# Three visits of 5, 4 and 5 attention chunks for two quads of heads, in place of four of 4, 3, 4 and 3

## The chip, the core and the metric

The kernel runs on one core of a Trainium2 chip. The metric is the device time of one launch in microseconds (us), the median of several runs. Engines are named as the profile names them: PE is TensorE (matmuls), DVE is VectorE, ACT is ScalarE, POOL is GpSimd, SP is SyncE, which here only issues transfers.

## What is computed

A sigmoid attention feeds a gated feed-forward layer. Eight batches of twelve heads, 448 positions, head width 64; the layer is 768 to 1536 to 768.

```python
scores = (1.0 / np.sqrt(64)) * np.matmul(q, k.transpose(0, 1, 3, 2)) - np.log(448)
attn = 1.0 / (1.0 + np.exp(-scores))
attn_out = np.matmul(attn, v)                        # (8, 12, 448, 64)
x = attn_out.transpose(0, 2, 1, 3).reshape(3584, 768)
g = x @ w_gate
out = (g * sigmoid(g) * (x @ w_val)) @ w_out
```

The sigmoid has no sum over a row, so a piece of the attention needs nothing from its neighbours. The kernel works on **quads**: four heads of one batch, 24 quads in all, three to a batch. The 448 keys of a quad are cut into seven **chunks** of 64. For a chunk, TensorE makes the scores of the four heads (`qk_tile`, four matmuls of 64x64 weights and 448 columns), and ScalarE takes their sigmoid (`sig_tile`). When all seven are there, TensorE multiplies them with the values (`pv`, 28 matmuls) and VectorE copies the result out as the layer's input.

## The kernel before

All matmul results go through four PSUM tiles of two banks each, handed out in turn: whoever asks next gets the tile that was handed out four requests ago, and must wait until that tile's last user has been read.

```python
ring = [psD.tile([128, 2, 512], FP32, tag=f"D{i}", name=f"ps_D{i}") for i in range(4)]

class Banked:
    def __init__(self, user=None, at=None, made=None):
        if at is None:
            at = ring_at[0] % 4
            ring_at[0] += 1
        k = ring_order[at]
        self.t = ring[k]
    # write(ins, bank) / read(ins, bank): say that an instruction touches one bank only,
    # so that it need not wait for the readers of the other one
```

Scores and their sigmoid. The score matmuls do not go through `write`, so the first of them waits until both banks of the tile have been read. A sigmoid can be split by bank, so that the next user of the tile gets its first bank sooner.

```python
def qk_tile(n, c, at=None):
    sd = Banked(at=at)
    ...
    for w in range(2):
        for h2 in range(2):
            nc.tensor.matmul(out=sc[w * 64:(w + 1) * 64, h2, :S], ...)     # 64x64 weights
    return sd

def sig_tile(n, c, sd, split=False):
    pt = pt_a[:, pt_at[0] % 10]
    if split:
        for h2 in range(2):
            sd.read(nc.scalar.activation(out=pt[:, h2, :], in_=sc[:, h2, :S], func=SIGM, ...), h2)
    else:
        nc.scalar.activation(out=pt, in_=sc[:, :, :S], func=SIGM, ...)
```

The product with the values takes a tile of the ring as well, and it too waits for both banks. Its three copies to `xT` run on VectorE (with `how` = 1, one of them on ScalarE).

```python
def pv(n, how=0, at=None):
    P = Banked(at=at).t
    for c in range(C):
        for h2 in range(2):
            for w in range(2):
                nc.tensor.matmul(out=P[g:g + 64, h2, :S], lhsT=vt[...], rhs=pts of (n, c), ...)
    first = nc.vector.tensor_copy(out=x, in_=P[:, 0, :S])
    ...
    done = [nc.vector.tensor_copy(out=o, in_=i) for o, i in halves[how:]]
```

Between the visits to the attention TensorE works on the layer. One `ffn1` is one slice of 128 of the 1536 columns for one batch: six matmuls for the gate into bank 0, six for the value into bank 1, then ScalarE and VectorE in a row.

```python
def ffn1(b, f):
    D = Banked("f", made=(b // 2, f))
    ffn1_mm(D, b, f, ...)                  # 6 matmuls gate -> bank 0, 6 matmuls value -> bank 1
    ffn1_gate(D, b, f)
    if b % 2:
        h_sums(b // 2, f)
        make_sums(budget[(b, f)])          # up to `budget` further sums on VectorE
    for fn in fill.pop((b, f), ()):        # further VectorE work in batches 4 and 5
        fn()

def ffn1_gate(D, b, f):
    s16 = ...; D.read(nc.scalar.activation(out=s16, in_=D.t[:, 0, :S], func=SIGM), 0)            # "s"
    t1 = ...;  D.read(nc.vector.tensor_tensor(out=t1, in0=D.t[:, 0, :S], in1=s16, op=MULT), 0)   # "t"
    D.read(nc.vector.scalar_tensor_tensor(out=hT[...], in0=D.t[:, 1, :S], ..., in1=t1, ...), 1)  # "hT"
```

The second half of the layer is `ffn2` (24 matmuls of 384 columns) and `ffn2_group` (42 of them). The last batches use `double`, a form with fewer matmuls, after the attention is over. `fill` puts `fast_w` and `x_sums`, VectorE work that prepares it, behind the `ffn1` of batches 4 and 5.

A **visit** is a group of chunks done together: the scores of its first two, then `pv` of a quad that was completed in an earlier visit, then the rest.

```python
visits = [tiles[:2], tiles[2:4]]
for i in range(0, len(tiles), C):
    visits += [tiles[i:i + 4], tiles[i + 4:i + C]] if i else [tiles[4:C]]

def attn_step(group, pvs, how):
    for part in (group[:2], group[2:]):
        scs = [(n, c, qk_tile(n, c)) for n, c in part]
        rest = [pv(pvs.pop(0), how) for _ in range(len(pvs))]
        for i, (n, c, sc) in enumerate(scs):
            sig_tile(n, c, sc, split=len(group) == 4 and part[0] == group[0] and i == 1)
        for f in rest:
            f()
```

A list of units (`ffn1`, `ffn2`, ...) with their estimated lengths is walked through, and a visit is put in when its planned time is reached and the last visit lies far enough back. `plan` hangs the loads, casts and transposes of later quads on chunks of earlier ones.

Of the kernel before, what the change touches and what calls it, by code (L numbers as in the profile page):

```python
# [20 lines left out]
def kernel(  # L21
# [13 lines left out]
    B, H, S, D = q.shape  # L35
    DM = H * D
    DFF = moe_w_gate.shape[1]
    C = S // D
    NJ = H // 4
    NP = H // 2  # L40
    NF = DFF // 128
    NQ = B * NJ
# [190 lines left out]
    def qk_tile(n, c, at=None):  # L233
        sd = Banked(at=at)
        sc = sd.t
        qt, kt = qT[(n, 0)], qT[(n, 1, c)]
        for w in range(2):
            for h2 in range(2):
                r = slice(h2 * 64, h2 * 64 + 64)
                nc.tensor.matmul(  # L240
                    out=sc[w * 64:(w + 1) * 64, h2, :S],
                    lhsT=kt[r, w * 64:(w + 1) * 64],
                    rhs=qt[r, :, w * 64:(w + 1) * 64],
                    start=True,
                    stop=True,
                )
        return sd

    def sig_tile(n, c, sd, split=False):
        sc = sd.t  # L250
        pt = pt_a[:, pt_at[0] % 10]
        pt_at[0] += 1
        if split:
            for h2 in range(2):
                sd.read(
                    nc.scalar.activation(out=pt[:, h2, :], in_=sc[:, h2, :S], func=SIGM, bias=sbias, scale=qkscale), h2
                )
        else:
            nc.scalar.activation(out=pt, in_=sc[:, :, :S], func=SIGM, bias=sbias, scale=qkscale)  # L259
        pts[(n, c)] = pt  # L260

    def pv(n, how=0, at=None):

        b, j = divmod(n, NJ)
        P = Banked(at=at).t
        vt = v16.pop(n)
        for c in range(C):
            pt = pts.pop((n, c))
            for h2 in range(2):
                for w in range(2):  # L270
                    r = slice(w * 64, w * 64 + 64)
                    g = (w ^ h2) * 64
                    nc.tensor.matmul(  # L273
                        out=P[g:g + 64, h2, :S],
                        lhsT=vt[r, h2, c * D:(c + 1) * D],
                        rhs=pt[r, h2, :],
                        start=(c == 0),
                        stop=(c == C - 1),
                    )

        def x_tile(h2):
            if n >= NQ - NJ:
                at = 4 * W2 + (2 * j + h2) * S
                return half_of(stg_a)[:, at:at + S]
            return xtp.tile([128, S], FP16, tag="xT", name=f"xT_{b}_{2 * j + h2}")

        x = x_tile(0)
        first = nc.vector.tensor_copy(out=x, in_=P[:, 0, :S])  # L288
        xT[(b, 2 * j)] = x
        x = x_tile(1)  # L290
        xT[(b, 2 * j + 1)] = x
        halves = [(x[w * 64:(w + 1) * 64, :], P[(1 - w) * 64:(2 - w) * 64, 1, :S]) for w in range(2)]
        done = [nc.vector.tensor_copy(out=o, in_=i) for o, i in halves[how:]]  # L293
        if how == 2:
            for o, i in halves:
                apart(nc.scalar.copy(out=o, in_=i), first)

        def rest():
            if how == 1:
                o, i = halves[0]  # L300
                apart(nc.scalar.copy(out=o, in_=i), first, *done)

        return rest
# [197 lines left out]
    budget = {}  # L501
# [10 lines left out]
    def make_sums(most):  # L512
        for _ in range(min(most, len(sumq))):
            pb, i, f, kind = sumq.pop(0)
            h1 = hT[(pb, f)].rearrange("p b s -> p (b s)")
            a11, a21 = h1[:, :GT], h1[:, GT:2 * GT]
            if kind in (1, 4):
                h2 = hT[(pb, f + FW)].rearrange("p b s -> p (b s)")
                a12, a22 = h2[:, :GT], h2[:, GT:2 * GT]
            t = htp.tile([128, GT], FP16, tag=f"S{kind}_{i}", bufs=1, name=f"S{kind}_{pb}_{i}")  # L520
            hS[(pb, kind, i)] = t
            if kind == 1:
                a, b, op = a21, a22, ADD
            elif kind == 2:
                a, b, op = hS[(pb, 1, i)], a11, SUB
            elif kind == 3:
                a, b, op = a11, a21, SUB
            else:
                a, b, op = a12, hS[(pb, 2, i)], SUB
            nc.vector.tensor_tensor(out=t, in0=a, in1=b, op=op)  # L530
# [119 lines left out]
    FU1, FU2, FU3, FU4 = 2.26, 3.9, 6.83, 7.85  # L650
    units = []
    f1_start, f1_end = {}, {}
# [25 lines left out]


    FIRST = f1_end[0] - 5.0  # L680
    PACE = ((2 * NJ, FIRST + 3.5), (3 * NJ, FIRST + 41.5), (3 * NJ + 2, FIRST + 60.5), (6 * NJ, f1_end[B - 5] - 1.0), (NQ, f1_end[B - 3] - 5.0))
    tiles = [(n, c) for n in range(NJ, NQ) for c in range(C)]
    visits = [tiles[:2], tiles[2:4]]
    for i in range(0, len(tiles), C):
        visits += [tiles[i:i + 4], tiles[i + 4:i + C]] if i else [tiles[4:C]]
    vtime = []
    for grp in visits:
        n, c = grp[0]
        b, j = divmod(n, NJ)
        if b == 1:  # L690
            vtime.append(4 * FU1 + (j * C + c) / (NJ * C) * (FIRST + 1.0 - 4 * FU1))
        else:
            at = n + (0.5 if c else 0.0)
            (n0, t0), (n1, t1) = [p for p in zip(PACE, PACE[1:]) if p[0][0] <= at][-1]
            vtime.append(t0 + (at - n0) / (n1 - n0) * (t1 - t0))

    def attn_step(group, pvs, how):
        for part in (group[:2], group[2:]):
            scs = [(n, c, qk_tile(n, c)) for n, c in part]
            rest = [pv(pvs.pop(0), how) for _ in range(len(pvs))]  # L700
            for i, (n, c, sc) in enumerate(scs):

                sig_tile(n, c, sc, split=len(group) == 4 and part[0] == group[0] and i == 1)
            for f in rest:
                f()

# [124 lines left out]
    for f, Df in enumerate(early):  # L831
# [7 lines left out]
    plan = {  # L839
        (3, 2): ((casts, 5), (post.append, 4)),  # L840
        (3, 4): ((post.append, 5),),
        (4, 0): ((fetch, 6),),
        (4, 4): ((ready, 6), (load_qk, 7), (load_qk, 8)),
        (5, 4): ((hold, 6), (load_v, 7), (w_out, 0)),
        (6, 0): ((ready, 7), (load_qk, 9)),
        (6, 4): ((hold, 7), (load_v, 8), (w_out, 1), (w_out, 2)),
        (7, 0): ((ready, 8), (load_qk, 10)),
# [1 line left out]
        (8, 0): ((ready, 9), (load_qk, 11)),  # L849
    }  # L850
    for n in range(8, NQ - 2):
        plan[(n, 4)] = ((ready, n + 2), (load_v, n + 2)) + ((load_qk, n + 4),) * (n + 4 < NQ)


    seq = []
    tcur = 3 * FU1
    since, was_v = 99.0, 9
    was, was_args = ffn1, (0, 2)
    for dur, fn, args in units:
        if visits and tcur >= vtime[0] and not (was is ffn1 and was_args[0] < 2 and was_args[1] == 0) and (vtime[0] < FIRST + 4 or since > (3.8 if len(visits[0]) > 3 else 2.0)):  # L860
            seq.append((None, visits.pop(0), 0 if fn is ffn1 else 1))
            vtime.pop(0)
            since, was_v = 0.0, 0
        seq.append((fn, args, not visits and was_v == 1))
        was, was_args = fn, args
        was_v += dur > 0.0
        since += dur
        tcur += dur

    for i, (fn, args, _) in enumerate(seq):  # L870
        if fn is ffn1:
            ahead = [len(a) if f is None else 0 for f, a, _ in seq[i + 1:i + 3]] + [0, 0]
            budget[args] = 3 if ahead[0] else 0 if ahead[1] == 4 else 2
        if fn is double:
            args[2].append(lambda: make_sums(5))

# [3 lines left out]
    for fn, args, how in seq:  # L880
        if fn is None:
            pvs, pend = pend, []
            attn_step(args, pvs, how)
            for n, c in args:
                for act, of in plan.get((n, c), ()):
                    act(of)
                if c == C - 1:
                    pend.append(n)
            while post:
                trans_pe(post.pop())  # L890
            continue
# [53 lines left out]
```

## Time and profile before

| | |
|---|---|
| time, median of 3 runs | 407.39 us (406.76 to 408.72) |
| span of the profiled execution | 405.0 us, TensorE's granted clock 0.998 |
| PE busy | 392.5 us (97%), 3140 matmuls |
| DVE busy | 266.5 us (66%) |
| ACT busy | 226.9 us (56%) |
| visits of the attention from quad 3 on | 43 |

A line of groups or of the timeline gives the kernel's line, the engine, the operation and its tiles (out<-in), with the start and the length in us or a count and the mean in ns; what stands in brackets is the time that the engine sat idle before it, and what ended that. L240 is the score matmul, L273 the product with the values, L314 `ffn1`, L629 and L571 `ffn2` and its group form, L437 the form of the last batches. L259 and L256 are the whole and the split sigmoid, L334, L336 and L340 are s, t and hT of `ffn1`, L288 and L293 the copies after `pv`.

### The profile page before, as it was taken

The numbers are of one execution on the slowest core, as the hardware profiler recorded it, in microseconds if no ns is written. First come the engines' busy times: TensorE is split into PE (matmuls) and PEld (weight loads), VectorE is DVE, ScalarE is ACT, GpSimd is POOL, SyncE is SP. The second block draws the span as 40 slices with busy tenths as digits, with TensorE's granted clock in tenths as the row PEclk, the third lists the DMA queues.
The fourth block names the chain that finished last, engine by engine and source line by source line (L and its number), as shares of the span: only waits on it lengthen the run. The fifth ranks groups of instructions, "written<-read, shape, count | busy, mean of one in ns | idle before, by whom it ended". The sixth has DMA issues, their size and how long they took to land.

```text
span 405.0 us, 7990 instructions
## 1 busy us (share of the span) xinstructions
PE 392.5 (97%) x3140; PEld 203.8 (50%) x3140; DVE 266.5 (66%) x508; ACT 226.9 (56%) x355; POOL 93.7 (23%) x121
## 2 busy tenths in 40 slices
PE   6799999999999999999999999999999999999995
PEld 3444544445555444444455554444555655555563
DVE  3737556678765555567764566889786558777753
ACT  5965885744444777777764547776650035666100
POOL 4528041424222232232200120000006950000000
PEclk9999999999999999999999999999999999999999
DMA  8999989899869997778717697000001440000135
GB/s 275 245 251 249 241 189 209 166 168 237 148 187 253 241 245 160 160 159 160 160 24 189 144 248 103 2 2 1 2 0 40 121 113 0 1 2 0 40 91 143
DMA packets 65284, 54.38 MB, mean 134 GB/s; under 512 B 35744, under 2 KB 61440, under 8 KB 65248
## 3 DMA queue, kind: packets, MB, share of 16 engines
q1 hardware_dynamic: 49744, 38.22, 39.3%
q0 software_dynamic: 15072, 15.34, 23.0%
q8 instruction: 24, 0.39, 0.4%
q10 hardware_dynamic: 432, 0.33, 0.3%
q14 instruction: 12, 0.10, 0.1%
HBM read 47.19 MB, written 11.01 MB: 144 GB/s over the span
## 4 chain that ended last, share of the span: by engine, by line
PE 90%; DVE 4%; DMA 3%; ACT 1%; issue 1%; SPq 0%; POOL 0%; DVEq 0%; ACTq 0%
PE ps_D L314 34%; PE ps_D L571 18%; PE ps_D L437 15%; PE ps_D L240 8%; PE ps_D L273 8%; PE ps_D L629 6%; DMA v<-in_v_dram 2%; DMA st<-in_q_dram 1%; DVE t L336 1%; DVE xT L293 1%; DVE xT L288 0%; PE ps_D L210 0%; ACT small L467 0%; DVE stg_a L384 0%; ACT snap L447 0%
## 5 line engine op out<-in xcount | busy, mean ns | idle before, releaser
L259 ACT ACTIVATE pt_a<-ps_D 128x896 f16<-128x896 f32 x148 | 127.2, 920 | 55.3 <-PE ps_D L240 49.2
L314 PE MATMUL ps_D<-xT,wg 128*128 128x448 f16 x360 | 79.4, 353 | 0.6 <-DVE t L336 0.5
L314 PE MATMUL ps_D<-xT,wv 128*128 128x448 f16 x360 | 78.9, 352 | 0.0
L191 POOL CAST c<-stg_a 128x896 bf16<-128x896 f32 x40 | 37.5, 945 | 130.8 <-DMA stg_a<-in_q_dram 118.4
L336 DVE TENSOR_TENSOR t<-ps_D,s 128x448 f16<-128x448 f32 x60 | 37.4, 623 | 43.7 <-ACT s L334 42.6
L314 PEld LDWEIGHTS <-wg 128*128 128x128 f16 x360 | 32.3, 98 | 39.4 <-issue 13.6
L314 PEld LDWEIGHTS <-wv 128*128 128x128 f16 x360 | 35.1, 98 | 33.0 <-issue 0.4
L334 ACT ACTIVATE s<-ps_D 128x448 f16<-128x448 f32 x60 | 33.1, 551 | 26.5 <-PE ps_D L314 26.5
L240 PE MATMUL ps_D<-T,T 64*64 64x448 bf16 x644 | 44.1, 357 | 2.1 <-DVE T L216 1.2
L447 ACT ACTIVATE snap<-ps_D 128x448 f32<-128x448 f32 x54 | 28.0, 542 | 31.8 <-DVE osb L582 20.7
L340 DVE SCALAR_TENSOR_TENSOR hT<-ps_D,t 128x448 f16<-128x448 f32 x60 | 37.5, 625 | 6.3
L273 PE MATMUL ps_D<-pt_a,v 64*64 64x448 f16 x672 | 35.9, 349 | 0.6 <-DMA v<-in_v_dram 0.6
L582 DVE TENSOR_SCALAR osb<-ps_D 128x384 f32<-128x384 f32 x43 | 24.0, 557 | 18.7 <-PE ps_D L571 18.5
L571 PEld LDWEIGHTS <-S 128*128 128x128 f16 x264 | 25.8, 98 | 17.7 <-issue 0.7
L571 PE MATMUL ps_D<-ramp_a,S 128*128 128x384 f16 x198 | 34.0, 326 | 0.5 <-DVE osb L582 0.5
L588 DVE SCALAR_TENSOR_TENSOR osb<-ps_D,osb 128x384 f32<-128x384 f32 x33 | 18.4, 557 | 13.4 <-PE ps_D L571 13.3
L240 PEld LDWEIGHTS <-T 64*64 64x64 bf16 x644 | 14.9, 105 | 24.5 <-issue 17.8
L273 PEld LDWEIGHTS <-v 64*64 64x64 f16 x672 | 19.4, 107 | 13.4 <-DMA v<-in_v_dram 1.0
L571 PEld LDWEIGHTS <-hT 128*128 128x128 f16 x198 | 19.0, 98 | 14.0 <-issue 1.8
L288 DVE CAST xT<-ps_D 128x448 f16<-128x448 f32 x21 | 13.1, 624 | 19.1 <-PE ps_D L273 17.4
L629 PE MATMUL ps_D<-wo,hT 128*128 128x384 f16 x144 | 24.6, 326 | 0.2 <-DVE hT L482 0.2
L437 PE MATMUL ps_D<-xS,wv 128*128 128x448 f16 x108 | 23.4, 352 | 0.3 <-DVE small L460 0.2
(98 smaller groups left out, 426.7 us busy)
## 6 DMA issues: line engine op xcount, KB each, us to landing
out_dram<-osb SPq DMA_DIRECT2D x52, 192.0 KB, 3.0
stg_a<-in_q_dram SPq DMA_DIRECT2D x18, 448.0 KB, 5.2
stg_a<-in_k_dram SPq DMA_DIRECT2D x18, 448.0 KB, 6.0
v<-in_v_dram POOLq DMA_DIRECT2D x24, 224.0 KB, 6.0
wg<-in_moe_w_gate_dram POOLq DMA_DIRECT2D x4, 576.0 KB, 11.9
wv<-in_moe_w_val_dram POOLq DMA_DIRECT2D x4, 576.0 KB, 12.9
wo<-in_moe_w_out_dram POOLq DMA_DIRECT2D x4, 576.0 KB, 10.1
stg_a<-in_q_dram POOLq DMA_DIRECT2D x3, 448.0 KB, 13.8
```

Of the source, the lines that this page charges most:

```text
L191: eng.tensor_copy(out=t.rearrange("p c h d -> p h c d"), in_=st.rearrange("p h (c d) -> p h c d", c=C))
L240: nc.tensor.matmul(out=sc[w * 64:(w + 1) * 64, h2, :S], lhsT=kt[r, w * 64:(w + 1) * 64], rhs=qt[r, :, w * 64:(w + 1) * 64], start=True, st ...
L259: nc.scalar.activation(out=pt, in_=sc[:, :, :S], func=SIGM, bias=sbias, scale=qkscale)
L273: nc.tensor.matmul(out=P[g:g + 64, h2, :S], lhsT=vt[r, h2, c * D:(c + 1) * D], rhs=pt[r, h2, :], start=(c == 0), stop=(c == C - 1),)
L314: nc.tensor.matmul(out=D.t[:, i, :S], lhsT=(wg16, wv16)[i][f // FW][:, pr, cs], rhs=xT[(b, pr)], start=(pr == 0), stop=(pr == NP - 1),),
L334: D.read(nc.scalar.activation(out=s16, in_=D.t[:, 0, :S], func=SIGM), 0)
L336: D.read(nc.vector.tensor_tensor(out=t1, in0=D.t[:, 0, :S], in1=s16, op=MULT), 0)
L340: nc.vector.scalar_tensor_tensor(out=hT[(b // 2, f)][:, b % 2, :], in0=D.t[:, 1, :S], scalar=hsc(b // 2), in1=t1, op0=MULT, op1=MULT),
L437: nc.tensor.matmul(out=D.t[:, bank, :S], lhsT=W(f, j), rhs=X(j), start=(start and j == 0), stop=(stop and j == JT - 1), skip_group_check=True,
L447: D.read(nc.scalar.mul(out=o, in_=D.t[:, bank, :S], mul=scale), bank)
L571: nc.tensor.matmul(out=D.t[:, bank, :hw], lhsT=l, rhs=B_(i), start=(first and i == 0), stop=(i == HF - 1), skip_group_check=True,),
L629: nc.tensor.matmul(out=D.t[:, half, :hw], lhsT=h[:, m * 128:(m + 1) * 128], rhs=wo16[f // FW][:, f % FW, half * hw:(half + 1) * hw], start ...
```

## The change

From quad 4 on, two quads (14 chunks) are done in three visits of 5, 4 and 5 chunks, where each quad had a visit of 4 and one of 3. The first visits (2, 2 and 3 chunks) stay. That makes 33 visits in place of 43: TensorE turns fewer times from the layer's full-width matmuls to the attention's 64x64 ones and back. A visit of 5 has three chunks ahead of `pv` and two behind it, and the third sigmoid is the split one; the visit of 4, which has no `pv` to do, splits its first. The times at which visits are due (`PACE`), the least distance between two and the extra sums behind an `ffn1` (`budget`) follow; for odd quads the loads and transposes of later quads move from chunk 4 to chunk 0.

```diff
-    PACE = ((2 * NJ, FIRST + 3.5), (3 * NJ, FIRST + 41.5), ...)
+    PACE = ((2 * NJ, FIRST + 3.5), (2 * NJ + 5 / C, FIRST + 15.0), (2 * NJ + 2, FIRST + 29.0), (3 * NJ, FIRST + 41.5), ...)
     tiles = [(n, c) for n in range(NJ, NQ) for c in range(C)]
-    visits = [tiles[:2], tiles[2:4]]
-    for i in range(0, len(tiles), C):
-        visits += [tiles[i:i + 4], tiles[i + 4:i + C]] if i else [tiles[4:C]]
+    visits, i = [], 0
+    for size in (2, 2, 3) + (5, 4, 5) * ((NQ - NJ - 1) // 2):
+        visits.append(tiles[i:i + size])
+        i += size
...
-            at = n + (0.5 if c else 0.0)
+            at = n + c / C
...
     def attn_step(group, pvs, how):
-        for part in (group[:2], group[2:]):
+        cut = 3 if len(group) > 4 else 2
+        late = cut - 1 if pvs else 0
+        for part in (group[:cut], group[cut:]):
             scs = [(n, c, qk_tile(n, c)) for n, c in part]
             rest = [pv(pvs.pop(0), how) for _ in range(len(pvs))]
             for i, (n, c, sc) in enumerate(scs):
-                sig_tile(n, c, sc, split=len(group) == 4 and part[0] == group[0] and i == 1)
+                sig_tile(n, c, sc, split=len(group) >= 4 and part[0] == group[0] and i == late)
...
     for n in range(8, NQ - 2):
-        plan[(n, 4)] = ((ready, n + 2), (load_v, n + 2)) + ((load_qk, n + 4),) * (n + 4 < NQ)
+        plan[(n, 0 if n % 2 else 4)] = ((ready, n + 2), (load_v, n + 2)) + ((load_qk, n + 4),) * (n + 4 < NQ)
...
-        if visits and tcur >= vtime[0] and not (...) and (vtime[0] < FIRST + 4 or since > (3.8 if len(visits[0]) > 3 else 2.0)):
+        if visits and tcur >= vtime[0] and not (...) and (vtime[0] < FIRST + 4 or since > 3.8):
...
-            budget[args] = 3 if ahead[0] else 0 if ahead[1] == 4 else 2
+            budget[args] = 3 if ahead[0] else 0 if ahead[1] > 3 else 2
```

In the order of the instructions the quiet middle of the kernel goes from

    visit(4, with pv)  ffn1  visit(3)  ffn1 ffn1          once for each quad

to

    visit(5, with pv)  ffn1 ffn1  visit(4)  ffn1 ffn1  visit(5, with pv)  ffn1 ffn1          once for two quads

More of the change, by code (lines that the diff above doesn't have):

```diff
@@ L680 @@
     FIRST = f1_end[0] - 5.0
-    PACE = ((2 * NJ, FIRST + 3.5), (3 * NJ, FIRST + 41.5), (3 * NJ + 2, FIRST + 60.5), (6 * NJ, f1_end[B - 5] - 1.0), (NQ, f1_end[B - 3] - 5.0))
+    PACE = ((2 * NJ, FIRST + 3.5), (2 * NJ + 5 / C, FIRST + 15.0), (2 * NJ + 2, FIRST + 29.0), (3 * NJ, FIRST + 41.5), (3 * NJ + 2, FIRST + 60.5), (6 * NJ, f1_end[B - 5] - 1.0), (NQ, f1_end[B - 3] - 5.0))
     tiles = [(n, c) for n in range(NJ, NQ) for c in range(C)]
-    visits = [tiles[:2], tiles[2:4]]
-    for i in range(0, len(tiles), C):
-        visits += [tiles[i:i + 4], tiles[i + 4:i + C]] if i else [tiles[4:C]]
+    visits, i = [], 0
+    for size in (2, 2, 3) + (5, 4, 5) * ((NQ - NJ - 1) // 2):
+        visits.append(tiles[i:i + size])
+        i += size
     vtime = []
@@ L690 @@
         if b == 1:
-            vtime.append(4 * FU1 + (j * C + c) / (NJ * C) * (FIRST + 1.0 - 4 * FU1))
+            vtime.append(4 * FU1 + (j * C + c) / (NJ * C) * (FIRST + 2.5 - 4 * FU1))
         else:
-            at = n + (0.5 if c else 0.0)
+            at = n + c / C
             (n0, t0), (n1, t1) = [p for p in zip(PACE, PACE[1:]) if p[0][0] <= at][-1]
@@ L859 @@
     for dur, fn, args in units:
-        if visits and tcur >= vtime[0] and not (was is ffn1 and was_args[0] < 2 and was_args[1] == 0) and (vtime[0] < FIRST + 4 or since > (3.8 if len(visits[0]) > 3 else 2.0)):
+        if visits and tcur >= vtime[0] and not (was is ffn1 and was_args[0] < 2 and was_args[1] == 0) and (vtime[0] < FIRST + 4 or since > 3.8):
             seq.append((None, visits.pop(0), 0 if fn is ffn1 else 1))
```

## Prediction

> **What bounds the kernel now.** I read the page first, its line of engines and its chain of work.
>
> ```profile
> PE 392.5 (97%) x3140; PEld 203.8 (50%) x3140; DVE 266.5 (66%) x508; ACT 226.9 (56%) x355; POOL 93.7 (23%) x121
> ...
> PE 90%; DVE 4%; DMA 3%; ACT 1%; issue 1%; SPq 0%; POOL 0%; DVEq 0%; ACTq 0%
> ```
>
> PE is busy for 97% of the span and carries 90% of the chain. Since a busy matmul row says little about waits, I read next what PE waited for between 137 and 209 us, some seven quads in the quiet middle.
>
> ```profile
> engine line waited for: us in total, times, longest us
> PE ps_D L314 <- DVE t L336: 0.3, 1, 0.3
> ```
>
> One wait of 0.3 us in 72 us: every four-request-old PSUM tile is free when PE asks for it. So PE's own stream sets the time, and the change can win only what the stream itself wastes. The chain, in order of time, shows one quad (start, length, line, matmuls):
>
> ```profile
> 157.07 0.50 PE ps_D L240 x8
> 157.57 1.32 PE ps_D L273 x28
> 158.90 0.38 PE ps_D L240 x8
> 159.27 2.38 PE ps_D L314 x12
> 161.65 0.69 PE ps_D L240 x12
> 162.34 4.65 PE ps_D L314 x24
> 166.99 0.50 PE ps_D L240 x8
> ```
>
> Two chunks take 0.50, three 0.69: a chunk is 0.19, and entering the attention costs 0.12. Twelve `ffn1` matmuls take 2.38, 24 take 4.65: an `ffn1` is 2.27 and coming back costs 0.11. Two chunks behind `pv` take 0.38, with no entry. A quad is then 3 x 2.27 + 7 x 0.19 + 1.32 + 2 x 0.23 = 9.92 us, and 166.99 - 157.07 is 9.92. A visit's own overhead is thus **0.23 us**.
>
> Next the timeline of the same stretch, for what the tiles wait on (start, length, engine):
>
> ```profile
> 155.97 0.54 ACT L334 ACTIVATE s<-ps_D 128x448 f16<-128x448 f32 x1 [0.90 <-PE ps_D L314]
> 156.55 0.62 DVE L336 TENSOR_TENSOR t<-ps_D,s 128x448 f16<-128x448 f32 x1
> ...
> 157.00 0.57 PE L240 MATMUL ps_D<-T,T 64*64 64x448 bf16 x8
> ...
> 157.28 0.63 DVE L340 SCALAR_TENSOR_TENSOR hT<-ps_D,t 128x448 f16<-128x448 f32 x1
> 157.40 1.49 PE L273 MATMUL ps_D<-pt_a,v 64*64 64x448 f16 x28
> ...
> 162.01 2.54 ACT L259 ACTIVATE pt_a<-ps_D 128x896 f16<-128x896 f32 x3 [0.72 <-PE ps_D L240]
> ...
> 164.42 0.56 ACT L334 ACTIVATE s<-ps_D 128x448 f16<-128x448 f32 x1
> ```
>
> The visit starts at 157.00, and `pv` at 157.40 behind two chunks. The hT of the `ffn1` just ended runs from 157.28 to 157.91, though its s began early, 1.03 before the visit. So the last `ffn1`'s tile is free only **0.91 us after a visit starts**, with ScalarE quite idle. After three sigmoids in a row s is late: it starts at 164.42, where its gate was ready at 163.42 + 0.2. The sigmoids follow each other every 0.81 (2.54 = 2 x 0.81 + 0.92), s follows the last one's start by 0.79, t follows s by 0.60, hT follows t by 0.73.
>
> Does a score matmul really wait for hT? One place shows it:
>
> ```profile
> 258.49 0.62 DVE L340 SCALAR_TENSOR_TENSOR hT<-ps_D,t 128x448 f16<-128x448 f32 x1
> ```
>
> ```profile
> 257.78 1.49 PE L273 MATMUL ps_D<-pt_a,v 64*64 64x448 f16 x28
> 259.17 0.57 PE L240 MATMUL ps_D<-T,T 64*64 64x448 bf16 x8
> ```
>
> hT (behind other VectorE work here) ends at 259.11 and the third chunk's scores start at 259.17, 1.39 after `pv` in place of the usual 1.33 (157.40 to 158.73). So the release takes 0.06.
>
> **What the Trainium skill says.** "TensorEngine Tiling (Array Packing)", Key Properties: changing the tiling mode drains TensorE; the trace agrees, with 0.12 in and 0.11 out. "PSUM — Partial Sum Buffer", Engine vs sequencer instructions: matmuls start and complete in program order; so a `pv` that waits holds everything behind it, and nothing later fills the gap. "Perfetto Trace Analysis", Identifying Performance Opportunities: a bubble that repeats on the engine that should be saturated can mean too few PSUM buffers; before has none in the middle, and that is what I expect to see afterwards. The same page, Tensor Engine Instruction: a matmul's end is an estimate; I therefore take waits from start to start.
>
> **The change, part by part.**
>
> *Removed:* ten visits of 43, 10 x 0.23 = **-2.3 us**. Matmuls, sigmoids and copies stay the same in number, so nothing else leaves PE. That is the whole gain, 0.6%.
>
> *Moved: which tile each request gets.* Let f be the last `ffn1` ahead of a visit; its tile is the fourth one asked for. Before, the visit of 4 asks chunk, chunk, `pv`, chunk: the fourth request comes behind `pv`, at 0.40 + 1.33 = 1.73 after the start, long after 0.91. The visit of 3 never gets that far. After, a visit of 5 asks chunk, chunk, chunk, `pv`: `pv` falls on f's tile at 0.40 + 0.19 = 0.59. And the visit of 4 has no `pv`, so its fourth chunk falls on f's tile at 0.59 too. The order of the instructions shows just this. Both wait until 0.91 + 0.06 = 0.97: **at least 0.38 us in every visit behind an `ffn1`.** This is a floor, with all other engines idle.
>
> *The visit of 5 behind a visit of 4* is worse. Count from the visit of 4: its fourth scores start at 0.97, the next `ffn1` at 1.26, two of them end and the visit of 5 starts at 1.26 + 4.65 = 5.91. Sigmoids start at 0.43 (split, 0.89), 1.32, 2.13, 2.94; the first s at 3.73, t 4.33, hT 5.06, the second t 0.54 later at 5.60, the second hT 6.33 to 6.95. `pv` wants 5.91 + 0.59 = 6.50 and gets 7.01: 0.51. Behind a visit of 5 with two `ffn1` I find the floor again, because ScalarE has caught up by the second s.
>
> *Sums.* (a) Quads 10 to 18, four rounds (four chunks, five, five): fours 4 x 0.38, fives after fours 4 x 0.51, fives after fives 4 x 0.38, together 5.1. (b) Quads 4 to 9: five visits at 0.38; the first five and the four after it have only one `ffn1` ahead of them and late sigmoids, 0.5 each; the four behind `ffn2` and its sums, guessed at 0.75; together 3.6. (c) Around `ffn2`: a group's last eviction (127.08 to 127.64, with the visit at 126.97) frees the tile at 0.73 against 0.59, five visits at 0.13; some six units find the third sigmoid of a five still in their tile, about 1.2 in all; off go 0.64 at 132.53 and 172.54, where an `ffn1` now waits for t, and some 0.5 of the kind at other groups: +0.7. (d) Quads 20 to 23: VectorE has `fast_w` (246.82 to the next start at 247.49, 0.67) and three `x_sums` (256.74 to 257.77, 1.03) between one hT and the next t. Before there is slack for that; afterwards it lands on the late pair: 0.38 + 1.15 + 0.85 + 0.5 + 1.0 = 3.9.
>
> (a) to (d) make 13.3, less 2.3: **+11.0 us**. The guesses in (b) and (d) add up each visit's worst order, and a wait in one visit gives ScalarE and VectorE time that the next one needs less; I take 2 off. 407.4 + 9 = **416.5 us**, 2.2% slower.
>
> **Rivals.** *The gain comes and no wait does: 405.1.* For it: PE has no wait in the middle today, the split third sigmoid and the longer distance between visits were made for such a ring, ACT is busy only 56%. Against: f's tile is held by work that cannot begin before f ends, and 0.59 lies ahead of 0.97 in any schedule. *ScalarE becomes the bound:* five sigmoids in 2.4 us of PE time. Two quads need 14 x 0.81 + 6 x 0.5 + 3 x 0.08 = 14.6 us of it in 20; it lags within a visit and catches up, so this is in (a), and by itself would add under 2. *Transfers come late:* the order of loads shifts for odd quads. Quad 7's transposed keys land at 72.1 (the hold on them ends there) and are used at 75.83; quad 8's 88.8 against 92.56. The loads run ahead of PE, held only by buffers, and the visits get later, not earlier; a loss here would be a single wait of 1 to 3 us, and I give it little. *The waits stack up:* if each late hT also delays the next visit's sigmoids, as in (d), for the whole middle, 420 and more.
>
> **Range and chances.** Floors alone: 24 visits begin behind an `ffn1` (16 with `pv`, 8 of 4 chunks); 24 x 0.38 = 9.1, less 2.3, gives 414.2. If a third of these floors fail to appear it is 411.2, and the full sum, 418.4, with some stacking is 420.5. Eight in ten: 411.5 to 420.5. The 2% line, 415.5, lies just below the middle of it: slower by over 2% 0.6, within 2% 0.38, faster by over 2% 0.02, since all that is removed is 0.6%.
>
> **What would show it.** PE's list of waits should name DVE hT L340 as what L273 waits for, some sixteen times, and for L240 some eight times. That list counts from the modelled end of the matmul before (at 132.53 it shows 0.22 idle where the start came 0.29 late), so I expect 6 to 9 us in sum there, for 9 to 13 from start to start; two quads in the middle should take 20.7 to 20.9 where two took 19.84; the longest waits should lie in the last four quads. It is wrong if those two lines are empty, if two quads take 19.6, if `pv` waits for a sigmoid or a transfer instead, or if the loss lies outside the attention's stretch, after the last `pv`, where I expect no more than 0.3 us either way.

## The result, and the profile after

| | before | after |
|---|---|---|
| time, median of 6 runs | 407.31 us (406.76 to 409.08) | 418.38 us (417.95 to 419.26) |
| ratio, 95% interval | 1 | 1.0262 (1.0238 to 1.0286) |
| span of the profiled execution | 405.0 us | 417.5 us |
| first score matmul behind the ramp to first matmul of L437 | 33.27 to 278.77: 245.50 us | 34.60 to 291.60: 257.00 us |
| from there to the end | 126.3 us | 125.9 us |

The change makes the kernel 2.6% slower. The fourth row is the stretch in which attention and `ffn1` take turns: it has grown by 11.50 us. What lies behind it has shrunk by 0.4, and 11.5 less 0.4 is the 11.1 by which the medians differ. Ahead of it the engines run the same instructions; the profiled execution of the changed kernel took 1.33 us longer there (34.60 against 33.27), but three later runs of it, changed only further on, begin the stretch at 33.27, 33.30 and 33.63, so this is not the change's. The loss lies where the visits are. In what follows, "the stretch" is this one, always taken from the profiled execution of a run.

The line of engines and the chain of work on the page of the changed kernel:

```profile
PE 398.1 (95%) x3140; PEld 212.4 (51%) x3140; DVE 268.0 (64%) x508; ACT 227.9 (55%) x365; POOL 94.2 (23%) x121
...
PE 70%; DVE 13%; ACT 8%; issue 5%; DMA 3%; DVEq 0%; SPq 0%; POOL 0%; ACTq 0%
```

PE is still busy for 95%, which would pass for healthy. Its share of the chain tells more: it falls from 90% to 70%, and what takes its place are DVE and ACT: they have come onto the path.

What PE waited for, in the whole changed kernel (us in sum, times, longest):

```profile
engine line waited for: us in total, times, longest us
PE ps_D L273 <- DVE hT L340: 5.9, 16, 1.0
PE ps_D L240 <- DVE hT L340: 2.1, 8, 0.6
```

Before, neither line existed. There are 16 waits of `pv` and 8 of score matmuls, as many as there are visits behind an `ffn1`. The list gives only the time that PE sat idle. Now two quads of the quiet middle in the timeline of the changed kernel:

```profile
152.43 0.76 PE L240 MATMUL ps_D<-T,T 64*64 64x448 bf16 x12
152.75 0.62 DVE L340 SCALAR_TENSOR_TENSOR hT<-ps_D,t 128x448 f16<-128x448 f32 x1
...
153.43 1.52 PE L273 MATMUL ps_D<-pt_a,v 64*64 64x448 f16 x28 [0.24 <-DVE hT L340]
...
154.75 0.57 PE L240 MATMUL ps_D<-T,T 64*64 64x448 bf16 x8
...
155.26 1.31 PE L314 MATMUL ps_D<-xT,wg 128*128 128x448 f16 x6
...
159.90 0.76 PE L240 MATMUL ps_D<-T,T 64*64 64x448 bf16 x12
160.23 0.62 DVE L340 SCALAR_TENSOR_TENSOR hT<-ps_D,t 128x448 f16<-128x448 f32 x1
...
160.91 0.38 PE L240 MATMUL ps_D<-T,T 64*64 64x448 bf16 x4 [0.24 <-DVE hT L340]
...
165.87 0.76 PE L240 MATMUL ps_D<-T,T 64*64 64x448 bf16 x12
...
166.88 1.52 PE L273 MATMUL ps_D<-pt_a,v 64*64 64x448 f16 x28 [0.26 <-DVE hT L340]
...
173.36 0.76 PE L240 MATMUL ps_D<-T,T 64*64 64x448 bf16 x12
```

The visit of 5 starts at 152.43, its `pv` at 153.43, 0.06 after the end of hT (152.75 + 0.62). With nothing to wait for it would have come at 0.59, so 0.41 is lost. The visit of 4 starts at 159.90, its fourth chunk at 160.91, again 0.06 behind an hT: 0.42. The next visit of 5 loses 0.42. From 152.43 to 173.36 two quads take 20.93 us, where they took 19.84.

### The profile page after: what moved, and what is told of

Read it like the earlier page. It is cut to its first block, busy times and chain, and to the rows that moved or that the text cites. A ratio compares the mean times of both kernels' runs of the same rounds, so it can differ in the third digit from the quotient of the medians.

```text
span 417.5 us, 8005 instructions
## 1 busy us (share of the span) xinstructions
PE 398.1 (95%) x3140; PEld 212.4 (51%) x3140; DVE 268.0 (64%) x508; ACT 227.9 (55%) x365; POOL 94.2 (23%) x121
## 4 chain that ended last, share of the span: by engine, by line
PE 70%; DVE 13%; ACT 8%; issue 5%; DMA 3%; DVEq 0%; SPq 0%; POOL 0%; ACTq 0%
PE ps_D L314 21%; PE ps_D L571 18%; PE ps_D L437 16%; PE ps_D L273 8%; DVE hT L340 4%; ACT pt_a L259 4%; DVE t L336 4%; PE ps_D L240 4%; PE ps_D L629 4%; ACT s L334 2%; DMA v<-in_v_dram 2%; DVE S L530 1%; DMA st<-in_q_dram 1%; DVE xT L293 1%; DVE ramp_a L498 1%
## 5 line engine op out<-in xcount | busy, mean ns | idle before, releaser
L259 ACT ACTIVATE pt_a<-ps_D 128x896 f16<-128x896 f32 x138 | 119.5, 931 | 43.4 <-PE ps_D L240 31.7
L240 PE MATMUL ps_D<-T,T 64*64 64x448 bf16 x644 | 45.1, 359 | 4.5 <-DVE hT L340 2.1
L447 ACT ACTIVATE snap<-ps_D 128x448 f32<-128x448 f32 x54 | 28.0, 542 | 31.1 <-DVE osb L582 20.7
L273 PE MATMUL ps_D<-pt_a,v 64*64 64x448 f16 x672 | 37.4, 358 | 6.6 <-DVE hT L340 5.9
L256 ACT ACTIVATE pt_a<-ps_D 128x448 f16<-128x448 f32 x60 | 29.4, 549 | 13.8 <-PE ps_D L240 13.8
L273 PEld LDWEIGHTS <-v 64*64 64x64 f16 x672 | 22.6, 107 | 20.6 <-issue 12.1
L240 PEld LDWEIGHTS <-T 64*64 64x64 bf16 x644 | 18.6, 106 | 26.6 <-issue 19.2
L588 DVE SCALAR_TENSOR_TENSOR osb<-ps_D,osb 128x384 f32<-128x384 f32 x33 | 18.4, 558 | 13.3 <-PE ps_D L571 13.2
```

What stands on the lines that cost most here:

```text
L240: nc.tensor.matmul(out=sc[w * 64:(w + 1) * 64, h2, :S], lhsT=kt[r, w * 64:(w + 1) * 64], rhs=qt[r, :, w * 64:(w + 1) * 64], start=True, st ...
L273: nc.tensor.matmul(out=P[g:g + 64, h2, :S], lhsT=vt[r, h2, c * D:(c + 1) * D], rhs=pt[r, h2, :], start=(c == 0), stop=(c == C - 1),)
```

## The experiments

The theory is the prediction's: the ring of four PSUM tiles hands the fourth request of a visit the tile of the `ffn1` that has just ended, and that tile is free only when its s, t and hT have run. The rivals are transfers that come late, ScalarE with its five sigmoids in a row, and VectorE work that happens to lie in between. The comparison in each run is with the kernel before, on the same chip.

### Everything but the grouping

```diff
-    for size in (2, 2, 3) + (5, 4, 5) * ((NQ - NJ - 1) // 2):
+    for size in (2, 2, 3) + (4, 3) * (NQ - NJ - 1):
...
-            at = n + c / C
+            at = n + (0.5 if c else 0.0)
...
-        late = cut - 1 if pvs else 0
+        late = 1
...
-    ... since > 3.8):
+    ... since > (3.8 if len(visits[0]) > 3 else 2.0)):
```

> Everything of the change stays (the due times, the least distance of the longer visits, the moved loads and transposes of odd quads, the budget of sums) but the grouping: visits of 4 and 3 again, cut after two chunks. Ring theory (the fourth request of a visit falls on the tile of the last ffn1): time as before, 407.3 within 0.5, no wait of L273 for hT. Rival transfers (the moved loads cost the time): 412 to 418, with waits of PE for transposed keys or v. Rival pacing (ffn1 and visits lie worse among each other): 409 or more.

Measured: 408.01 us, where the kernel before had 406.75 beside it, ratio 1.0023 (1.0011 to 1.0036): more than the half microsecond allowed, and far below the 412 of late transfers. The stretch is 246.94, 1.44 over before. In it there is no wait for hT, none for keys or values. The 1.4 us are one event, which the timeline of this run shows:

```profile
85.78 2.12 DVE L530 TENSOR_TENSOR S<-S,hT 128x384 f16<-128x384 f16 x1
85.87 3.82 POOL L191 CAST c<-stg_a 128x896 bf16<-128x896 f32 x4
...
89.50 1.30 PE L314 MATMUL ps_D<-xT,wg 128*128 128x448 f16 x6 [1.55 <-DVE t L336]
```

One of the sums on VectorE, usually 0.36 us, takes 2.12 while GpSimd runs four casts, and the `ffn1` behind the next visit waits 1.55 for the t that this holds up. PE waits for no transfer there; whether the new due times or the moved loads brought the sum and the casts together is not shown. The changed kernel has no such wait. So the rest of the change costs at most these 1.4 us, and 10 or more of the 11.5 belong to the grouping.

### hT made later, in both kernels

```diff
         D.read(nc.vector.tensor_tensor(out=t1, ..., op=MULT), 0)
+        if b in (1, 2):
+            nc.vector.tensor_tensor(out=s16, in0=t1, in1=t1, op=ADD)      # unused
```

The same line goes into the kernel before and into the changed one.

> The kernel before, with one more VectorE instruction (an unused sum of t with itself, 128x448 in fp16, about 0.33 us) between t and hT of the 24 ffn1 of batches 1 and 2, so that hT ends some 0.33 us later there. Ring theory: in the kernel before the fourth request comes 1.73 us after the start of a visit and hT would end at 1.24, so nothing is lost: ratio 1.000, within 0.3 us. Rival (any later hT costs time, since VectorE's chain bounds these stages anyway): plus 0.33 us for a good part of the 24, 4 us or more.

> The changed kernel with the same extra VectorE instruction between t and hT in the 24 ffn1 of batches 1 and 2. Ring theory: the nine or ten visits that follow one of these ffn1 wait 0.33 us longer each: plus 3.0 to 3.5 us over the changed kernel's 418.4, so about 421.6, and the waits of L273 and L240 for hT grow from 0.2 idle to 0.5 in those visits alone. Rival ScalarE (the five sigmoids in a row make everything late, hT has room): 418.4, unchanged.

Measured: before with it 407.73, ratio 1.0017 (1.0005 to 1.0028); after with it 421.21, ratio 1.0349 (1.0319 to 1.0378). The stretch of before grows by 1.23, of which one wait of 0.92 again stands behind a 2.12 us VectorE instruction beside GpSimd's casts (at 89.60), here the added one itself; not one other visit behind the lengthened `ffn1` waits for hT. So the 4 us of the rival do not appear, and what is over the 0.3 us allowed is the added instruction's own long case. The stretch of the changed kernel grows by 2.55. Its timeline, in a visit of 4:

```profile
160.66 0.76 PE L240 MATMUL ps_D<-T,T 64*64 64x448 bf16 x12
160.87 0.39 DVE L338 TENSOR_TENSOR s<-t 128x448 f16<-128x448 f16 x1
...
161.18 0.62 DVE L342 SCALAR_TENSOR_TENSOR hT<-ps_D,t 128x448 f16<-128x448 f32 x1
...
161.85 0.38 PE L240 MATMUL ps_D<-T,T 64*64 64x448 bf16 x4 [0.43 <-DVE hT L342]
```

The added instruction runs from 160.87 to 161.26, hT follows, ends at 161.80, and the fourth chunk starts at 161.85, 1.19 after the visit in place of 1.01. The nine visits behind such an `ffn1` are later by 0.18 to 0.65 each, 2.46 in sum against the same visits of the changed kernel, which is nearly all of the 2.55; the visits behind other `ffn1` stay within 0.11 of what they were. So hT's end sets when these visits go on. My 0.33 was too large: t leaves a gap of 0.11 ahead of hT anyway, the extra instruction fills it, and hT is only about 0.2 later in most.

### ScalarE taken out of the way

```diff
-        s16 = tmp.tile([128, S], FP16, tag="s16", name="s16")
-        D.read(nc.scalar.activation(out=s16, in_=D.t[:, 0, :S], func=SIGM), 0)
...
-        D.read(nc.vector.tensor_tensor(out=t1, in0=D.t[:, 0, :S], in1=s16, op=MULT), 0)
+        D.read(nc.vector.tensor_copy(out=t1, in_=D.t[:, 0, :S]), 0)
```

This leaves out the sigmoid of the gate in all 60 `ffn1`; its time shows only what remains when nothing in `ffn1` waits for ScalarE.

> The changed kernel without the ScalarE step of ffn1: t is a plain copy of the gate, so the sigmoid of the gate is left out of the 60 ffn1, and hT no longer waits for ScalarE at all. Ring theory with its floor: hT still cannot start before the value matmuls end, and ends some 0.75 after the visit starts in place of 0.91; the 24 waits shrink by about 0.2 each and the long ones of the last four quads to the floor too, but all 24 stay: 410.5 to 413. Rival (ScalarE's five sigmoids in a row are the cause): with no s behind them every one of the 24 waits is gone, 405 to 407.

Measured: 412.06, ratio 1.0122 (1.0084 to 1.0159); the stretch shrinks by 6.38. PE's list of waits names hT no more, which looks like the rival's victory. The timeline, from start to start, says otherwise:

```profile
149.71 0.76 PE L240 MATMUL ps_D<-T,T 64*64 64x448 bf16 x12
149.82 0.62 DVE L338 SCALAR_TENSOR_TENSOR hT<-ps_D,t 128x448 f16<-128x448 f32 x1 [0.51 <-PE ps_D L314]
...
150.50 1.52 PE L273 MATMUL ps_D<-pt_a,v 64*64 64x448 f16 x28
...
157.05 1.17 PE L240 MATMUL ps_D<-T,T 64*64 64x448 bf16 x16
158.15 1.31 PE L314 MATMUL ps_D<-xT,wg 128*128 128x448 f16 x6
```

`pv` comes 0.79 after the visit's start, not 0.59; four chunks take 1.10 to the next `ffn1`, not 0.88. All 24 visits behind an `ffn1` still lose about 0.20 (one 0.25). The list doesn't show it because it counts from the modelled end of the matmul before, and a `pv` normally starts 0.17 ahead of that end. What is left is hT's own: it waits for the last matmuls of `ffn1`, starts 0.11 after the visit and takes 0.62. So about half of the 0.41 stays without ScalarE. The other half comes with s, but little of it from sigmoids that make s late. In the changed kernel, ahead of the visit at 152.43:

```profile
151.45 0.54 ACT L334 ACTIVATE s<-ps_D 128x448 f16<-128x448 f32 x1 [1.22 <-issue]
```

This s starts 0.98 ahead of its visit, behind an idle ScalarE; in the kernel before it was 1.03 (155.97, visit at 157.00). It is the time that s and t take in a row that holds hT back.

### Another cut

```diff
-        cut = 3 if len(group) > 4 else 2
+        cut = 2
```

> The changed kernel with the cut of a visit of 5 after two chunks in place of three (and the second sigmoid split): chunk, chunk, pv, then three chunks. Now pv falls on the tile of the last but one ffn1 and the third chunk on that of the last, 1.7 us after the start. Ring theory: the sixteen waits of L273 for hT vanish, the eight of L240 in the visits of 4 stay; but the ring holds as few tiles as before, so new waits come: the fifth chunk for the second sigmoid (0.16), the next ffn1 for the copies out of pv's tile (0.07 and 0.14), about 0.4 in all for each visit of 5. Time 418.4 within 2. Rival (only the order of pv is at fault, and a better order gives the gain): 409 to 412. Rival ScalarE: 418.4 with the waits of pv still there.

Measured: 441.66, ratio 1.0842 (1.0811 to 1.0872), the stretch 23.74 longer than that of the changed kernel. The moves were as expected: `pv` now starts 0.40 after each visit without a wait, and the eight waits of the visits of 4 stay. The price was not: I had said within 2 us of 418.4. PE's waits of this run:

```profile
PE ps_D L314 <- DVE xT L293: 22.0, 15, 2.6
...
PE ps_D L240 <- DVE hT L340: 1.8, 8, 0.3
```

The next `ffn1` now takes `pv`'s tile, and PE sits idle for 1.24 or more until all three copies to `xT` are done, the last of which ends 1.9 us after the first starts. I had let the gate go after the first copy, since it needs one bank only; but the copies behind `pv` are not registered by bank, so its first matmul waits for the last of them. The cut after three chunks keeps two scores and one whole `ffn1` between `pv` and the next user of its tile. A wait was exchanged for one some three times as long.

### VectorE's extra work moved

```diff
-    (-2, h + 1, w2[:1]), (-2, h + 2, w2[1:2]), (-2, h + 3, xs2[:3]), (-2, h + 4, xs2[3:6]),
-    (-2, h + 5, xs2[6:9]), (-1, h, xs2[9:]), (-1, h + 2, w2[2:3]), (-1, h + 3, w2[3:4]),
+    (-2, h + 1, w2[:1]), (-2, h + 3, w2[1:2] + xs2[:3]),
+    (-2, h + 5, xs2[3:9]), (-1, h + 1, xs2[9:]), (-1, h + 3, w2[2:4]),
```

The longest waits of the changed kernel lie in the last quads. Its timeline at the longest:

```profile
258.93 0.62 DVE L340 SCALAR_TENSOR_TENSOR hT<-ps_D,t 128x448 f16<-128x448 f32 x1
259.47 0.75 DVE L384 TENSOR_TENSOR wv<-wv,wg 128x1152 f16<-128x1152 f16 x1
...
259.75 0.76 PE L240 MATMUL ps_D<-T,T 64*64 64x448 bf16 x12
...
260.86 0.62 DVE L340 SCALAR_TENSOR_TENSOR hT<-ps_D,t 128x448 f16<-128x448 f32 x1
...
261.54 1.33 PE L273 MATMUL ps_D<-pt_a,v 64*64 64x448 f16 x24 [1.03 <-DVE hT L340]
```

Between the hT at 258.93 and the t ahead of the next hT lies `fast_w` (L384), 0.75; `pv` comes 1.79 after the visit's start.

> The changed kernel with the VectorE work that prepares the last batches moved, in batches 4 and 5, from the first ffn1 behind a visit to the last one ahead of the next visit, so that it no longer lies between one hT and the next t. Prediction's part (d): the three long waits of L273 (1.03, 0.77, 0.87 idle) and the 0.29 of L240 fall to 0.2 to 0.3, minus 1.8 to 2.2 us, 416.4. Rival (the long waits come from the sigmoids, or VectorE only shifts its backlog to the end of the attention): within 0.5 of 418.4.

Measured: 416.97, ratio 1.0220 (1.0181 to 1.0260); the stretch is 1.32 shorter. PE's waits of this run:

```profile
PE ps_D L273 <- DVE hT L340: 4.1, 16, 0.4
PE ps_D L240 <- DVE hT L340: 2.1, 8, 0.5
```

The counts are the same, 16 and 8, but the sum for `pv` falls from 5.9 to 4.1. The four late visits lose 0.54, 0.42, 0.41 and 0.43 from start to start in place of 1.20, 0.94, 0.47 and 1.05: 1.87 less. Most of the other half microsecond was given back around batch 1, where a wait of 0.26 is new and another one 0.13 longer. The intervals of this ratio and of the changed kernel's overlap; it is these visits in the trace that show the effect. So part (d) is, beyond the floor, VectorE's backlog, and can be cured; the floor stays, and the kernel is still slower than the one before.

### The gain by itself

```diff
-        visits += [tiles[i:i + 4], tiles[i + 4:i + C]] if i else [tiles[4:C]]
+        more = 7 * C <= i < 15 * C                       # quads 10 to 17: visits of 4, 2 and 1
+        visits += ([tiles[i:i + 4], tiles[i + 4:i + 6], tiles[i + 6:i + C]] if more else [...]) if i else [tiles[4:C]]
...
```

> The kernel before with the visit of 3 of quads 10 to 17 cut into one of 2 and one of 1, each behind one ffn1: eight visits more, and no request on a tile that is not yet free. It measures the gain that the change was made for, by itself: 8 x 0.23 = 1.8 us, ratio 1.0045, no new wait of L240 or L273. Rival (a turn to the attention and back is hidden, or costs what the profile cannot show): below 0.5 us, or above 4.

The due times and the least distance of these visits are changed with it.

Measured: 408.57, ratio 1.0030 (1.0013 to 1.0046), the stretch 1.29 longer. No wait for hT. One of the eight places, from a visit of 2 to the next visit of 4:

```profile
142.26 0.57 PE L240 MATMUL ps_D<-T,T 64*64 64x448 bf16 x8
...
147.83 0.57 PE L240 MATMUL ps_D<-T,T 64*64 64x448 bf16 x8
```

That is 5.57, at all eight, where the kernel before takes 5.34 from the visit of 3 to the next (141.74 to 147.08) when nothing waits: **0.23 for a visit**, 1.84 in all. The ratio stays below the 1.0045 expected because the two waits for t that before has at 132.53 and 172.54 (0.64 from start to start) are gone here: behind a visit of 2 the next `ffn1` is the third request and no longer falls on the tile of the last one. So the change bought ten times 0.23, 2.3 us.

### What these waits point to

The kernel before has three waits of its own in the stretch: two for t (0.22 and 0.28 idle) and one of 0.47 for an eviction held up behind a sum on VectorE. From its list of PE's waits:

```profile
PE ps_D L314 <- DVE t L336: 0.5, 2, 0.3
PE ps_D L571 <- DVE osb L582: 0.5, 1, 0.5
```

Both have to do with order alone.

```diff
-        for prs in (range(NP - 2), range(NP - 2, NP)) if f == 0 else (range(NP),):
+        for prs in (range(NP - 2), range(NP - 2, NP)) if f == 0 and b == 1 else (range(NP),):
```

> The kernel before, where the first ffn1 of a batch takes its twelve matmuls in the plain order in batches 0, 2 and 3 too (gate, then value), because their inputs are long there; only batch 1 keeps the order with the last two inputs at the end. The two waits for t at the second ffn1 of batches 2 and 3 (0.22 and 0.28 idle) should go: minus 0.6 us, ratio 0.9985, faster than both kernels if so. Rival: the wait moves to the next request and the ratio is 1.000.

Measured: 406.44, ratio 0.9987 (0.9968 to 1.0006): the two waits are gone from the list and the stretch is 0.83 shorter, but the interval holds 1. With the second order as well:

```diff
-    o_units += ts[:4] + [(FU2, ffn2, (pb, 0))] + ts[4:7] + [(FU2, ffn2, (pb, 3))] + ts[7:]
+    o_units += ts[:4] + [(FU2, ffn2, (pb, 0))] + ts[4:] + [(FU2, ffn2, (pb, 3))]
```

> The kernel before with two orders changed and the visits of 4 and 3 kept: the first ffn1 of batches 0, 2 and 3 takes gate, then value, as in the run before this one, and the last of the eight sums over the output weights on VectorE moves from behind the visit at 109.6 us to ahead of it, where VectorE idles, so that it no longer delays an eviction (0.47 idle of L571 at 114.37). Theory (these waits of PE are real time): minus 0.64 and minus 0.6, 406.0 to 406.3, ratio 0.997, faster than both kernels. Rival (noise, or the waits move on): 1.000.

Measured: 406.07, **ratio 0.9958 (0.9943 to 0.9974)**, the stretch 244.27, 1.23 shorter than before; the three waits are gone from PE's list. This is faster than both kernels, if by little: the medians, 407.33 and 406.07, differ by 1.26, which is what the stretch says.

## Why the prediction was right

The measured 418.4 lies in the range, and on the side of 2% that had the larger chance. By its steps:

**The gain, 2.3 us.** Right: 0.23 for each visit in the run with more of them.

**Which tile each request gets, and the floor of 0.38.** Right in place and number: 24 visits behind an `ffn1`, 24 waits for hT, where the list should show some sixteen and eight. In 18 of them 0.36 to 0.43 is lost, 12.2 us in all 24 from start to start, where the list shows 8.0 (9 to 13 and 6 to 9 were forecast), and two quads take 20.93, against 20.7 to 20.9; in the middle mostly 0.41, because s and hT run some 0.04 later against the visit than in the kernel before (why, is not shown). That hT's end sets it is shown by the run with hT later. It is a floor for the chain of s, t and hT: without s, 0.20 is left.

One step of the account is missing. The visit of 3 in the kernel before doesn't ask for a fourth tile, but the `ffn1` behind it does: it falls on the last `ffn1`'s tile too, only 0.69 after the visit's start, well ahead of 0.97. The kernel before:

```profile
161.58 0.76 PE L240 MATMUL ps_D<-T,T 64*64 64x448 bf16 x12
...
162.06 0.62 DVE L340 SCALAR_TENSOR_TENSOR hT<-ps_D,t 128x448 f16<-128x448 f32 x1
...
162.27 1.31 PE L314 MATMUL ps_D<-xT,wg 128*128 128x448 f16 x6
```

It starts 0.41 before hT ends (162.68), since its matmuls are registered by bank: those for the gate need bank 0 only, which t has read. The two waits for t in the kernel before are this same request, where t is late. So the place in the ring is half of the story; the other half is that score matmuls and `pv` wait for both banks.

**Fives behind fours, 0.51.** The mechanism was seen in the trace (s is late behind four sigmoids, and the second hT runs 0.34 to 0.96 after the visit's start), but it costs 0.42 and no more, but for one of 0.54. The visit of 5 was reckoned to start 5.91 after the visit of 4. Where the visit of 4 loses 0.36 it does, and 0.54 is lost (138.92 to 144.83); where the visit of 4 loses 0.41 it starts 5.97 after it (159.90 to 165.87), and ScalarE and VectorE have used that time.

**The sums.** From start to start, each less 0.59: (a) 5.1 as predicted; (b) 3.9 for 3.6, the largest 0.85 behind `ffn2`, where 0.75 was guessed; the five visits of (c) 0.64 for 0.65; (d) 4.0 for 3.9. Together 13.7, where the list of the prediction makes 13.3. Less 2.3 that is 11.4, and the stretch has grown by 11.5. The other terms of (c), 1.2 more and 1.1 less, were not measured one by one; only their balance, nearly nothing, is borne out.

**The step that failed is "I take 2 off".** The reason given, that a wait in one visit gives ScalarE and VectorE time that the next one needs less, holds for the fives behind fours, where it is worth 0.1 a visit. It does not touch the floor, which comes anew with the `ffn1` just ahead of each visit. The sum before this step, 407.4 + 11.0 = 418.4, was the measured time. That it meets the tenth is luck: (b) was 0.3 too small, and the time after the attention 0.4 too large.

**The rivals.** Transfers: no wait of PE for keys or values in the whole stretch, and the run with everything but the grouping puts the rest of the change at 1.4 us at the most, in one VectorE event. ScalarE as the bound, with five sigmoids in a row: s in the middle is late by 0.05, and with s gone 24 losses of 0.20 stay. Waits that stack up: they don't; in the middle each round of three visits loses what the one before it lost. After the attention 0.4 less was found, where no more than 0.3 either way was expected.

What stays open: nothing tried here removes the floor and keeps the ten visits saved. A cut after two chunks with the copies of `pv` registered by bank was not tried. Nor was a `pv` whose matmuls are registered by bank and take bank 0 first. By an estimate from these traces its 28 matmuls last 1.32 us, so bank 1 would be needed only 0.66 after its start, 1.25 after the visit's, when hT has long read it (0.97); that would free the visits of 5, not those of 4.

## What to carry to other kernels

When buffers go round in a ring, write down for each request which earlier user holds its slot and when that user can be done at the earliest; a regrouping that leaves all work unchanged moves this by a place, and here one place cost some 0.4 us or more at 24 visits, for a saving of 0.23 ten times. Write down too whether the request needs the whole slot at once or only the part that comes free first. An engine in the chain with time to spare (ACT at 55%) says nothing against such a wait, since it is the latency of s, t and hT in a row and not their throughput. Measure a wait from start to start: a list of idle times hid 24 waits of 0.20 completely.

## What was not expected of the hardware

One of the sums on VectorE, with two fp16 inputs in SBUF, takes 0.36 us at the median, and about 1 us at places where GpSimd casts run beside it, in both kernels (0.97 at 93.76 before). In two of the runs such an instruction took 2.12, long enough to hold up PE. The Trainium skill, "SBUF — State Buffer", Who interferes with whom, states that such an instruction contends with a GpSimd instruction that reads SBUF, and that one of them then blocks; these runs agree, and add that it may be held past two of four casts in a row (0.93 us each where a cast runs alone). PE starts 0.05 to 0.06 us after the end of the read it waits for: at each of the 24 waits for hT in the changed kernel, and at the 20 for the copies behind `pv` in the run with the other cut.
